# PSUM banks of attention from one list of free banks, with a new order of the attention words

## The chip, the cores and the metric

The kernel runs on one core of a Trainium2 chip. The metric is the device time of one execution in microseconds (us), the median of several runs; lower is better.

## What is computed

The reference chains three blocks on two sequences (B = 2) of S = 448 tokens with DM = 768 channels (12 heads of D = 64):

```python
scores = matmul(q, k^T) / sqrt(64); scores[j > i] = -1e9          # causal attention
attn = exp(scores - rowmax); attn = attn / (rowsum + 1e-9); x = attn @ v
h = relu(x^T @ w_tok1) @ w_tok2; u = x + h^T                      # mixing over tokens, 448 -> 256 -> 448
x = u + relu(u @ w_ch1) @ w_ch2                                   # MLP over channels, 768 -> 1536 -> 768
u = x + real(fft2(x)); un = normalised u                          # Fourier mixing
out = u + relu(un @ w_ch1b) @ w_ch2b                              # MLP, 768 -> 3072 -> 768
```

Inputs are 64-bit floats. The kernel turns each weight into a high and a low part (fp32r) and makes three matmuls for one product: high by high, low by high, high by low.

## The kernel before

The program has five stages; the change concerns the first, which holds the attention, the token mixing, the conversion of the first weights and the first six tiles of the first MLP. Its work is cut into 571 "words", a letter with numbers. The string `ORDER` lists them in one hand-written order, and `tc.manual_schedule` puts each word's instructions on its engines in just that order. Every engine takes its own instructions strictly in that order; between engines only data and buffers make one wait. The rest of the program has its own order and is not changed.

Heads are worked in 12 pairs n = 0 to 11; three pairs make a half (0 to 3). The words that this text speaks of:

- `K`n loads q and k of pair n, `V`n loads v, `R`k loads raw weight k, all as DMAs from SyncE's queue (SP). `e`n.p scales q (VectorE, pairs 0 to 2). `k`, `l`, `q`, `m` split k and q in high and low (pairs 3 and up).
- `S`n.g (scores, L350) makes one group of score rows of both heads on TensorE (PE) into two neighbouring PSUM banks. Pair 0 has four groups, the others three. `N`n.i (maxima, L379, VectorE) and `E`n.i (exps, L387, ScalarE) then work on row block i and read those banks. Group 0 of pairs 1 and up holds row blocks 0 and 1.
- `T`n.u (transposes, L400, PE, four small transposes into one bank), `C`n.u (pt_copy, L413: ScalarE for u = 1 and 3, VectorE else) brings them to SBUF; `P`n (pv, L419, PE) multiplies by v, `O`n (pv_copy, ScalarE), `X`n (rows, L439, PE transposes), `x`n (divide, L450, VectorE) writes the attention result of the pair into the tile `x32` of its half, of which there is one buffer for all halves.
- `h`, `g` split that result; `A`h.t (mix_in, PE, 12 matmuls), `r`, `s`; `B`h.p (channels, L504, PE) transposes pair p of half h out of `x32`, `b` copies it; `D`h.p (mix_out, PE, 6 matmuls), `d`, `u`, `w`.
- `W`k.j is step j of the conversion of weight k (0: ScalarE, 1 to 3: VectorE, 4: ScalarE, 5: GpSimd). `U`f (18 matmuls) and `Y`x (12) are tiles of the first MLP on PE, `y`, `z`, `a` read them.

PSUM has eight banks, the tile `psum`. In attention they are dealt out by two fixed rings, independent of what is free. `ybank` (L209) goes round banks 0 to 3 and serves T, P, X, A, B and D (and, two at a time by `ypair`, groups 2 and 3 of pair 0). `spair` (L217) alternates between banks 4, 5 and banks 6, 7 and serves all other S, and U and Y through `sbank`, which uses one of the two. A word that writes a bank waits until the last reader of that bank is done. After attention `bank` (L221) goes round all eight.

Of the kernel before, what the change touches and what calls it, by code (L numbers as in the profile page):

```python
# [70 lines left out]

ORDER = """K0 e0.0 S0.0 e0.1 K1 N0.0 E0.0 S0.1 N0.1 K2 S0.2 e1.0 N0.2 S0.3 N0.3 E0.1 e1.1 e2.0 S1.0 V0 N1.1
S1.1 E0.2 K3 E0.3 N1.0 T0.2 T0.4 T0.3 E1.0 E1.1 N1.2 E1.2 C0.2 T0.0 Z0 V1 T0.1 e2.1 C0.4 S1.2 C0.1 C0.0 k3
R0 S2.0 l3 C0.3 P0 N1.3 q3 E1.3 N2.1 K4 T1.0 S2.1 N2.0 E2.1 m3 Z1 O0 T1.2 C1.0 N2.2 T1.4 X0 E2.0 S2.2 E2.2
W0.0 T1.1 C1.2 C1.1 C1.4 q4 x0 S3.0 T1.3 N2.3 N3.1 C1.3 E2.3 P1 N3.0 E3.0 S3.1 T2.2 E3.1 O1 T2.0 k4 W0.1 R1
T2.4 S3.2 T2.3 m4 W1.0 N3.2 C2.2 T2.1 V3 C2.3 C2.1 l4 V2 C2.0 E3.2 C2.4 X1 N3.3 W0.2 W0.3 P2 S4.0 B0.0 E3.3
T3.2 O2 x1 K5 N4.0 T3.0 N4.1 T3.3 W0.4 C3.2 b0.0 S4.1 T3.4 C3.0 T3.1 E4.1 B0.1 W1.1 E4.0 C3.4 S4.2 C3.3 k5
C3.1 h0 Z2 P3 W0.5 X2 b0.1 q5 l5 g0 N4.2 N4.3 E4.2 m5 S5.0 E4.3 S5.1 x2 T4.3 Z4 W1.2 Z3 T4.4 C4.4 O3 h1 T4.1
h2 T4.0 C4.3 T4.2 C4.0 C4.2 N5.0 X3 K6 C4.1 k6 N5.2 N5.1 B0.2 g2 g1 R2 W2.0 q6 A0.1 A0.0 x3 V5 V4 W1.3 W2.1
E5.0 E5.1 S5.2 l6 m6 E5.2 S6.0 W1.4 K7 r0.0 N5.3 P4 E5.3 S6.1 N6.0 N6.1 s0.0 r0.1 b0.2 T5.4 O4 k7 s0.1 X4  # L80
T5.1 T5.0 C5.4 T5.2 E6.0 E6.1 x4 W1.5 D0.0 C5.1 D0.1 N6.2 C5.0 T5.3 W2.2 S6.2 E6.2 q7 h3 l7 m7 S7.0 d0.1
C5.2 K8 q8 C5.3 P5 N6.3 R3 k8 h4 N7.0 E6.3 N7.1 d0.0 T6.4 T6.2 T6.0 E7.0 E7.1 S7.1 S7.2 O5 T6.3 l8 g4 V6 K9
C6.3 k9 C6.2 C6.4 B1.1 X5 C6.0 T6.1 D0.2 N7.2 m8 q9 Z5 x5 N7.3 W2.3 b1.1 B1.2 C6.1 B1.0 P6 Z6 d0.2 E7.2 S8.0
N8.0 N8.1 h5 E7.3 T7.3 O6 b1.2 T7.0 b1.0 T7.2 C7.3 T7.4 T7.1 C7.0 X6 E8.0 E8.1 S8.1 S8.2 C7.1 W2.4 Z7 g5 g3
C7.2 A1.1 C7.4 A1.0 x6 N8.2 B2.0 N8.3 W3.0 W3.1 W3.2 E8.2 l9 m9 S9.0 E8.3 S9.1 V7 P7 V8 K10 r1.1 s1.1 u0.1
h6 W2.5 Z8 u0.0 r1.0 s1.0 N9.0 T8.0 W3.3 T8.1 b2.0 T8.3 q10 u0.2 k10 R4 W4.0 N9.1 E9.0 O7 X7 C8.1 C8.0 T8.4
E9.1 C8.3 D1.0 x7 B2.1 T8.2 N9.2 S9.2 m10 E9.2 l10 w0.1 S10.0 C8.4 d1.0 C8.2 P8 b2.1 N9.3 E9.3 T9.2 T9.1
D1.1 W3.4 O8 h7 K11 q11 T9.0 W4.1 N10.0 N10.1 W4.2 C9.2 T9.3 C9.1 T9.4 E10.0 C9.3 E10.1 d1.1 X8 C9.0 D1.2
S10.1 S10.2 m11 x8 h8 k11 C9.4 V9 P9 V11 Z9 u1.0 N10.2 E10.2 N10.3 E10.3 d1.2 O9 W3.5 l11 S11.0 S11.1 B2.2
R5 W5.0 b2.2 T10.1 C10.1 T10.0 T10.2 g7 g8 w0.2 w0.0 g6 N11.0 N11.2 N11.1 T10.3 C10.3 u1.2 E11.0 A2.0 r2.0  # L90
C10.2 C10.0 X9 T10.4 W4.3 A2.1 W5.1 x9 W5.2 W4.4 E11.1 S11.2 s2.0 V10 C10.4 P10 N11.3 u1.1 E11.2 r2.1 s2.1
E11.3 T11.2 C11.2 T11.0 C11.0 T11.1 O10 T11.4 T11.3 W5.3 C11.4 X10 W4.5 R6 W6.0 W6.1 Z10 R7 C11.1 C11.3 P11
w1.2 D2.0 O11 X11 x10 D2.2 d2.2 Z11 x11 h10 d2.0 B3.1 b3.1 u2.0 h9 W5.4 w1.1 w1.0 U0 g10 B3.2 U1 W6.2 u2.2
y0 b3.2 h11 B3.0 y1 W5.5 W7.0 W7.1 W6.3 W6.4 g9 g11 A3.0 A3.1 z0 D2.1 b3.0 r3.0 s3.0 W7.2 z1 W7.3 r3.1 s3.1
U2 y2 D3.0 D3.1 d3.0 z2 d3.1 W7.4 U3 W6.5 W7.5 w2.2 w2.0 d2.1 u3.0 u2.1 w3.0 w2.1 D3.2 y3 z3 u3.1 d3.2 Y0
w3.1 u3.2 w3.2 a0 Y1 a1
"""
# [7 lines left out]
def fused_kernel(ctx: ExitStack, tc: tile.TileContext, qk, v, w1, w2, wa, wb, wc, wd, fa, fb, out):  # L105
# [97 lines left out]

    def take(ring, n):
        k = turn[ring] % n
        turn[ring] += 1
        return k

    def ybank():  # L209
        return psum[:, take("y", 4)]  # L210

    def ypair():
        k = take("y", 4)
        take("y", 4)
        return psum[:, k : k + 2]

    def spair():  # L217
        k = 4 + 2 * take("s", 2)
        return psum[:, k : k + 2]
# [807 lines left out]
```

## Time and profile before

| | |
|---|---|
| median of 3 runs | 684.19 us (683.26 to 685.48) |
| the profiled execution | 683.87 us, span of its instructions 682.0 us |
| PE busy | 676.6 us, 99% of the span |
| VectorE (DVE) busy | 533.6 us, 78% |
| ScalarE (ACT) busy | 288.8 us, 42% |
| GpSimd (POOL) busy | 122.4 us, 18% |

The attention stage is the first 151 us or so of the span: its last matmuls are those of `Y1`, which start at 148.6 us. A matmul's record runs on past the start of the next one, since matmuls are pipelined; what a group of matmuls costs is therefore read from its first start to the first start of the group behind it. In the rows below, a word can be found by its line: L363 with L377 is S, L408 T, L425 P, L444 X, L489 A, L507 B, L520 D. L385 is N, L395 E, L417 C, L457 x, L343 V, L335 e, L154 W.3.

### The profile page before, as it was taken

To read this page: it belongs to the slowest core of one execution; us is meant where nothing else is said; L and a number is where in the kernel's file an instruction comes from. 1 tells how busy PE (TensorE), PEld (TensorE's weight loads), DVE (VectorE), ACT (ScalarE), POOL (GpSimd) and SP (SyncE) were. 2 spreads that over 40 slices of the span, in tenths; PEclk is the share of its full clock that TensorE was granted. 3 is DMA by queue.
4 is the path that set the end of the run, shared out by engine and by line. 5 is a ranking of instruction groups with operands and counts; after the bars stand their busy time and mean duration, and the time that the engine had idled before them with its cause. 6 is when DMAs were issued, how large, how long until landed. Compare 5 with 4: busy or idle time off the path is not lost.

```text
span 682.0 us, 10238 instructions
## 1 busy us (share of the span) xinstructions
PE 676.6 (99%) x3922; PEld 618.9 (91%) x3922; DVE 533.6 (78%) x888; ACT 288.8 (42%) x619; POOL 122.4 (18%) x102
## 2 busy tenths in 40 slices
...
PEclk9999999999999999999999999999999999999999
...
GB/s 226 113 128 116 115 88 63 78 213 142 131 152 110 109 125 92 93 1 1 93 93 94 125 153 93 99 90 151 124 93 93 175 113 145 93 92 76 111 46 55
DMA packets 20865, 73.38 MB, mean 108 GB/s; under 512 B 2366, under 2 KB 7230, under 8 KB 20448
## 3 DMA queue, kind: packets, MB, share of 16 engines
...
HBM read 69.96 MB, written 2.75 MB: 107 GB/s over the span
## 4 chain that ended last, share of the span: by engine, by line
PE 98%; DVE 1%; ACT 0%; DMA 0%; issue 0%; SPq 0%; DVEq 0%
PE psum L259 13%; PE psum L239 13%; PE psum L263 13%; PE psum L264 13%; PE psum L238 13%; PE psum L240 13%; PE psum L363 4%; PE psum L408 3%; PE psum L425 3%; PE psum L489 3%; PE psum L520 2%; PE psum L718 2%; PE psum L787 1%; PE psum L444 1%; PE psum L507 1%; PE psum L377 1%
## 5 line engine op out<-in xcount | busy, mean ns | idle before, releaser
L259 PE MATMUL psum<-gh,wh 128*128 128x448 f32 x432 | 157.5, 365 | 0.0
L239 PE MATMUL psum<-acth,wl 128*128 128x448 f32 x432 | 156.8, 363 | 0.0
L264 PE MATMUL psum<-gl,wh 128*128 128x448 f32 x432 | 156.6, 363 | 0.0
L263 PE MATMUL psum<-gh,wl 128*128 128x448 f32 x432 | 156.6, 362 | 0.0
L238 PE MATMUL psum<-acth,wh 128*128 128x448 f32 x432 | 156.6, 362 | 0.0
L240 PE MATMUL psum<-actl,wh 128*128 128x448 f32 x432 | 156.0, 361 | 0.0
L143 ACT ACTIVATE m<-w 128x512 f32<-128x512 f32 (+2 forms) x92 | 70.9, 772 | 121.0 <-DVE wl L163 87.0
L161 ACT CAST wh<-m 128x512 fp32r<-128x512 f32 (+1 forms) x90 | 63.3, 704 | 91.4 <-PE psum L264 55.3
L264 PEld LDWEIGHTS psum<-gl,wh 128*128 128x128 f32 x432 | 81.0, 188 | 6.0
L238 PEld LDWEIGHTS psum<-acth,wh 128*128 128x128 f32 x432 | 81.0, 188 | 5.9
L263 PEld LDWEIGHTS psum<-gh,wl 128*128 128x128 f32 x432 | 81.0, 188 | 5.7 <-issue 0.2
L259 PEld LDWEIGHTS psum<-gh,wh 128*128 128x128 f32 x432 | 81.1, 188 | 5.6 <-issue 0.2
L239 PEld LDWEIGHTS psum<-acth,wl 128*128 128x128 f32 x432 | 81.1, 188 | 5.0
L240 PEld LDWEIGHTS psum<-actl,wh 128*128 128x128 f32 x432 | 80.9, 187 | 5.2
L163 DVE TENSOR_TENSOR wl<-m,wh 128x512 fp32r<-128x512 f32 (+1 forms) x84 | 69.5, 830 | 14.0 <-ACT wh L161 13.7
L150 DVE SCALAR_TENSOR_TENSOR m<-w,m 128x512 uint32<-128x512 uint32 (+2 forms) x92 | 78.5, 853 | 2.2
L145 DVE TENSOR_SCALAR m<-m 128x512 f32<-128x512 f32 (+2 forms) x92 | 51.0, 554 | 36.9 <-ACT m L143 36.9
L154 DVE SCALAR_TENSOR_TENSOR m<-w,m 128x512 uint32<-128x512 uint32 (+2 forms) x92 | 78.1, 850 | 1.8
L244 ACT ACTIVATE gh<-psum 128x448 fp32r<-128x448 f32 x72 | 37.8, 540 | 74.1 <-PE psum L240 73.8
L246 DVE SCALAR_TENSOR_TENSOR gl<-psum,gh 128x448 fp32r<-128x448 f32 x72 | 43.8, 619 | 29.1 <-ACT gh L244 29.1
L395 ACT ACTIVATE p<-psum,nmx 112x112 f32<-112x112 f32 (+3 forms) x96 | 46.5, 502 | 10.2 <-DVE nmx L385 10.1
L146 DVE TENSOR_SCALAR m<-m 128x512 uint32<-128x512 uint32 (+2 forms) x92 | 48.0, 522 | 2.6
(160 smaller groups left out, 812.0 us busy)
## 6 DMA issues: line engine op xcount, KB each, us to landing
...
```

The source lines that it names most:

```text
L143: act.activation(out=m, in_=hi.bitcast(F32), func=AF.Abs)
L145: vec.tensor_scalar(out=m, in0=m, scalar1=F64_MIN, scalar2=F64_MAX, op0=ALU.max, op1=ALU.min)
L150: vec.scalar_tensor_tensor(out=mu, in0=lo, scalar=29, in1=mu, op0=ALU.logical_shift_right, op1=ALU.bitwise_or)
L154: vec.scalar_tensor_tensor(out=mu, in0=hi, scalar=0xC0000000, in1=mu, op0=ALU.bitwise_and, op1=ALU.bitwise_or)
L161: act.copy(wh, m)
L163: low_engine[0].tensor_tensor(out=wl, in0=m, in1=f(wh), op=ALU.subtract)
L238: mm(pb[:, :S], lhsT=lh, rhs=act_h[ct][b], start=ct == 0, stop=False)
L239: mm(pb[:, :S], lhsT=ll, rhs=act_h[ct][b], start=False, stop=False)
L240: tail[0] = mm(pb[:, :S], lhsT=lh, rhs=act_l[ct][b], start=False, stop=ct == NCT - 1).ins
L259: mm(pb[:, :S], lhsT=lh, rhs=gh, start=j + k == 0 and seeded is None, stop=False, skip_group_check=seeded is not None,)
L263: mm(pb[:, :S], lhsT=ll, rhs=gh, start=False, stop=False, skip_group_check=seeded is not None)
L264: tail[0] = mm(pb[:, :S], lhsT=lh, rhs=gl, start=False, stop=j == last and k == nk - 1, skip_group_check=seeded is not None,).ins
```

## The change

The two fixed rings go. One list, `ring`, holds the free banks in the order in which they came free. `grab` takes from it the bank that has been free for longest, with a preference: a single bank is looked for among banks 0 to 3 first and a pair (an even bank and its neighbour) among banks 4 to 7, where a bank of the other side counts as freed `FAR` = 4 places later. `drop`, called by the word that reads a bank last, puts it back at the end. All this happens while the program is written, in the order of the words: a bank counts as free as soon as its last reading word stands earlier in `ORDER`. U and Y now take one bank and not one of two. `bank`, after attention, goes round the eight banks in the order in which the list ends up.

`exps` drops the pair of its score group, `pt_copy` the bank of T, and so on for P, X, A, B, D, U and Y.

With it comes a new `ORDER` of the same 571 words. The diff, cut to its core (the lines of `ORDER` shown are those around the start, around P1 and P2, and around T4.2):

```diff
+FAR = 4
...
-ORDER = """K0 e0.0 S0.0 e0.1 K1 N0.0 E0.0 S0.1 N0.1 K2 S0.2 e1.0 N0.2 S0.3 N0.3 E0.1 e1.1 e2.0 S1.0 V0 N1.1
-S1.1 E0.2 K3 E0.3 N1.0 T0.2 T0.4 T0.3 E1.0 E1.1 N1.2 E1.2 C0.2 T0.0 Z0 V1 T0.1 e2.1 C0.4 S1.2 C0.1 C0.0 k3
...
-W0.0 T1.1 C1.2 C1.1 C1.4 q4 x0 S3.0 T1.3 N2.3 N3.1 C1.3 E2.3 P1 N3.0 E3.0 S3.1 T2.2 E3.1 O1 T2.0 k4 W0.1 R1
-T2.4 S3.2 T2.3 m4 W1.0 N3.2 C2.2 T2.1 V3 C2.3 C2.1 l4 V2 C2.0 E3.2 C2.4 X1 N3.3 W0.2 W0.3 P2 S4.0 B0.0 E3.3
...
-h2 T4.0 C4.3 T4.2 C4.0 C4.2 N5.0 X3 K6 C4.1 k6 N5.2 N5.1 B0.2 g2 g1 R2 W2.0 q6 A0.1 A0.0 x3 V5 V4 W1.3 W2.1
-E5.0 E5.1 S5.2 l6 m6 E5.2 S6.0 W1.4 K7 r0.0 N5.3 P4 E5.3 S6.1 N6.0 N6.1 s0.0 r0.1 b0.2 T5.4 O4 k7 s0.1 X4
...
+ORDER = """K0 K1 e0.0 S0.1 S0.0 e0.1 N0.1 N0.0 E0.1 S0.2 e1.1 e1.0 S0.3 N0.2 V0 E0.0 S1.1 N0.3 S1.0 E0.2 N1.2 E0.3 E1.2
+N1.0 K2 S1.2 T0.2 K3 N1.1 T0.4 T0.0 e2.1 T0.1 E1.0 C0.2 E1.1 e2.0 C0.1 T0.3 S2.1 C0.4 q3 C0.0 N1.3 C0.3 k3 S2.0
+m3 E1.3 P0 N2.2 Z1 T1.1 N2.0 T1.2 R0 T1.4 E2.2 l3 T1.0 O0 K4 V1 N2.1 X0 C1.2 E2.1 T1.3 E2.0 W0.0 C1.0 S2.2 C1.4
+C1.3 V3 Z0 x0 N2.3 q4 S3.0 S3.1 N3.0 N3.2 C1.1 E2.3 E3.2 P1 O1 T2.0 T2.1 W0.1 T2.4 h0 R1 k4 S3.2 T2.3 l4 N3.1
+E3.1 C2.0 C2.4 T2.2 C2.1 N3.3 C2.3 C2.2 X1 V2 K5 W0.2 m4 E3.0 E3.3 k5 P2 x1 T3.4 T3.3 Z2 T3.0 W1.0 B0.1 T3.1
...
+E4.0 Z3 P3 x2 E4.3 O3 V5 K6 W1.1 h2 S5.0 W0.5 S5.1 B0.0 b0.0 N5.1 T4.1 C4.1 g1 T4.3 k6 N5.0 q6 g2 N5.2 m6 X3 R2
+E5.1 E5.0 A0.1 A0.0 r0.1 T4.4 T4.0 V4 C4.3 W1.2 E5.2 B0.2 x3 r0.0 l6 W1.3 T4.2 W1.4 C4.4 S5.2 W2.0 C4.0 C4.2 K7
+s0.1 q7 S6.0 N5.3 R3 b0.2 s0.0 k7 W1.5 E5.3 N6.0 S6.1 Z4 l7 N6.2 P4 K8 m7 S6.2 D0.0 h3 N6.1 E6.2 T5.0 N6.3 T5.2
...
-    turn = dict(y=0, s=0, all=0)
+    ring = list(range(8))
+    turn = [0]
+    held = {}
...
+    def grab(key, uses=1, n=1):
+        old = {b: i + FAR * ((b < 4) == (n == 2)) for i, b in enumerate(ring)}
+        if n == 2:
+            old = {b: max(old[b], old[b + 1]) for b in range(0, 8, 2) if b in old and b + 1 in old}
+        b = min(old, key=old.get)
+        k = list(range(b, b + n))
+        for b in k:
+            ring.remove(b)
+        held[key] = k, [uses]
+        return psum[:, k[0]] if n == 1 else psum[:, k[0] : k[0] + 2]
+
+    def drop(key):
+        k, left = held[key]
+        left[0] -= 1
+        if not left[0]:
+            ring.extend(k)
+
     def bank():
-        return psum[:, take("all", 8)]
+        turn[0] += 1
+        return psum[:, ring[(turn[0] - 1) % 8]]
...
-            sp = c.sp[g] = spair() if n or g < 2 else ypair()
+            sp = c.sp[g] = grab(("S", n, g), 1 if g or not n else 2, 2)
...
+            drop(("S", n, g))
...
-            tv = c.tv[u] = ybank()
+            tv = c.tv[u] = grab(("T", n, u))
...
+            drop(("T", n, u))
```

## Rows read from the trace of the kernel before

**Rows 1.** The page, parts 1 and 2: PE's busy time, and its granted clock.

```profile
PE 676.6 (99%) x3922; PEld 618.9 (91%) x3922; DVE 533.6 (78%) x888; ACT 288.8 (42%) x619; POOL 122.4 (18%) x102
PEclk9999999999999999999999999999999999999999
```

**Rows 2.** All waits of PE: who waited for whom, us, times, longest.

```profile
PE psum L197 <- PEq L1014: 0.8, 1, 0.8
PE psum L363 <- DVE resid L335: 0.6, 1, 0.6
PE psum L363 <- DMA resid<-in_qk: 0.2, 1, 0.2
```

**Rows 3.** Stretches: length, busy PE, PEld, DVE, ACT, POOL (instructions), clock, DMA.

```profile
0.00:17.00 17.00, 15.41 (x130) 11.49 (x130) 12.09 (x30) 12.89 (x46) 4.17 (x15) 1.00 0.81 226
34.00:51.00 17.00, 17.00 (x154) 14.05 (x154) 15.81 (x29) 14.53 (x41) 8.69 (x7) 1.00 0.39 128
51.00:68.00 17.00, 17.00 (x162) 14.36 (x160) 13.71 (x25) 14.50 (x47) 3.55 (x3) 1.00 0.35 116
```

**Rows 4.** Timeline of PE (start, us, what): score groups alone, and one behind another.

```profile
23.61 0.41 PE L363 MATMUL psum<-kh,qh 64*112 64x336 f32 x2
...
24.37 1.36 PE L408 MATMUL psum<-ident,p 112*112 112x112 f32 x12
25.66 0.46 PE L363 MATMUL psum<-kh,qh 64*112 64x448 f32 x2
...
26.55 0.98 PE L408 MATMUL psum<-ident,p 112*112 112x112 f32 x8
27.37 0.60 PE L444 MATMUL psum<-ident,ots 128*112 128x128 f32 x4
...
73.47 0.41 PE L363 MATMUL psum<-kh,qh 64*112 64x336 f32 x2
...
74.11 0.44 PE L363 MATMUL psum<-kh,qh 64*112 64x448 f32 x2
...
79.78 0.38 PE L363 MATMUL psum<-kh,qh 64*112 64x256 f32 x2
...
80.70 0.39 PE L363 MATMUL psum<-kh,qh 64*112 64x336 f32 x2
...
81.42 2.11 PE L425 MATMUL psum<-pt,v 112*64 112x448 f32 x16
```

**Rows 5.** Timeline of PE: S1.0 and S1.1, then S5.0, S5.1 and T4.3.

```profile
7.13 0.81 PE L363 MATMUL psum<-resid,resid 64*112 64x112 f32 x8
...
8.77 0.82 PE L363 MATMUL psum<-resid,resid 64*112 64x336 f32 x4 [0.64 <-DVE resid L335]
...
38.60 0.49 PE L363 MATMUL psum<-kh,qh 64*112 64x256 f32 x2
...
39.75 0.60 PE L363 MATMUL psum<-kh,qh 64*112 64x336 f32 x2
...
40.69 2.13 PE L408 MATMUL psum<-ident,p 112*112 112x112 f32 x20
42.66 0.60 PE L444 MATMUL psum<-ident,ots 128*112 128x128 f32 x4
```

**Rows 6.** The load of v: timeline (V2's issue, P2's start), and all twelve landings.

```profile
23.72 0.33 SPq L343 DMA_DIRECT2D v<-in_v  x1
28.06 2.30 PE L425 MATMUL psum<-pt,v 112*64 112x448 f32 x16
DMA to landing us min/median/max: 2.5/4.3/5.6
```

**Rows 7.** Timeline of DVE: two C4, then x3, W1.3 and W2.1.

```profile
42.48 1.16 DVE L417 COPY pt<-psum 112x448 f32<-112x448 f32 x2
45.14 0.68 DVE L457 TENSOR_TENSOR x<-psum,ssum 112x512 f32<-112x512 f32 x1
45.74 1.08 DVE L154 SCALAR_TENSOR_TENSOR m<-w,m 128x896 uint32<-128x896 uint32 x1
46.73 0.56 DVE L145 TENSOR_SCALAR m<-m 128x768 f32<-128x768 f32 x1
```

**Rows 8.** Timeline of PE: B0.2, then A0.1 and A0.0 up to S5.2.

```profile
43.10 0.55 PE L507 MATMUL psum<-ident,x 112*128 112x112 f32 x4
43.41 0.94 PE L489 MATMUL psum<-xh,w1h 112*128 112x384 f32 x4
...
47.80 0.46 PE L363 MATMUL psum<-kh,qh 64*112 64x448 f32 x2
```

More of the change, by code (lines that the diff above doesn't have):

```diff
@@ L69 @@
 ENGINES = {getattr(mybir.EngineType, e) for e in ("PE", "DVE", "Activation", "Pool", "SP")}
-ORDER = """K0 e0.0 S0.0 e0.1 K1 N0.0 E0.0 S0.1 N0.1 K2 S0.2 e1.0 N0.2 S0.3 N0.3 E0.1 e1.1 e2.0 S1.0 V0 N1.1
-S1.1 E0.2 K3 E0.3 N1.0 T0.2 T0.4 T0.3 E1.0 E1.1 N1.2 E1.2 C0.2 T0.0 Z0 V1 T0.1 e2.1 C0.4 S1.2 C0.1 C0.0 k3
-R0 S2.0 l3 C0.3 P0 N1.3 q3 E1.3 N2.1 K4 T1.0 S2.1 N2.0 E2.1 m3 Z1 O0 T1.2 C1.0 N2.2 T1.4 X0 E2.0 S2.2 E2.2
-W0.0 T1.1 C1.2 C1.1 C1.4 q4 x0 S3.0 T1.3 N2.3 N3.1 C1.3 E2.3 P1 N3.0 E3.0 S3.1 T2.2 E3.1 O1 T2.0 k4 W0.1 R1
@@ L76 @@
-T2.4 S3.2 T2.3 m4 W1.0 N3.2 C2.2 T2.1 V3 C2.3 C2.1 l4 V2 C2.0 E3.2 C2.4 X1 N3.3 W0.2 W0.3 P2 S4.0 B0.0 E3.3
-T3.2 O2 x1 K5 N4.0 T3.0 N4.1 T3.3 W0.4 C3.2 b0.0 S4.1 T3.4 C3.0 T3.1 E4.1 B0.1 W1.1 E4.0 C3.4 S4.2 C3.3 k5
-C3.1 h0 Z2 P3 W0.5 X2 b0.1 q5 l5 g0 N4.2 N4.3 E4.2 m5 S5.0 E4.3 S5.1 x2 T4.3 Z4 W1.2 Z3 T4.4 C4.4 O3 h1 T4.1
-h2 T4.0 C4.3 T4.2 C4.0 C4.2 N5.0 X3 K6 C4.1 k6 N5.2 N5.1 B0.2 g2 g1 R2 W2.0 q6 A0.1 A0.0 x3 V5 V4 W1.3 W2.1
-E5.0 E5.1 S5.2 l6 m6 E5.2 S6.0 W1.4 K7 r0.0 N5.3 P4 E5.3 S6.1 N6.0 N6.1 s0.0 r0.1 b0.2 T5.4 O4 k7 s0.1 X4
@@ L81 @@
[L81 to L95, printed above, removed]
@@ L96 @@
-w3.1 u3.2 w3.2 a0 Y1 a1
+ORDER = """K0 K1 e0.0 S0.1 S0.0 e0.1 N0.1 N0.0 E0.1 S0.2 e1.1 e1.0 S0.3 N0.2 V0 E0.0 S1.1 N0.3 S1.0 E0.2 N1.2 E0.3 E1.2
[3 more added lines that the diff above has]
+E3.1 C2.0 C2.4 T2.2 C2.1 N3.3 C2.3 C2.2 X1 V2 K5 W0.2 m4 E3.0 E3.3 k5 P2 x1 T3.4 T3.3 Z2 T3.0 W1.0 B0.1 T3.1
@@ new lines @@
+C3.4 O2 h1 b0.1 C3.1 W0.3 C3.3 T3.2 C3.0 q5 W0.4 X2 S4.0 C3.2 N4.1 E4.1 S4.1 N4.2 m5 N4.0 l5 S4.2 g0 N4.3 E4.2
+E4.0 Z3 P3 x2 E4.3 O3 V5 K6 W1.1 h2 S5.0 W0.5 S5.1 B0.0 b0.0 N5.1 T4.1 C4.1 g1 T4.3 k6 N5.0 q6 g2 N5.2 m6 X3 R2
+E5.1 E5.0 A0.1 A0.0 r0.1 T4.4 T4.0 V4 C4.3 W1.2 E5.2 B0.2 x3 r0.0 l6 W1.3 T4.2 W1.4 C4.4 S5.2 W2.0 C4.0 C4.2 K7
+s0.1 q7 S6.0 N5.3 R3 b0.2 s0.0 k7 W1.5 E5.3 N6.0 S6.1 Z4 l7 N6.2 P4 K8 m7 S6.2 D0.0 h3 N6.1 E6.2 T5.0 N6.3 T5.2
+E6.0 O4 E6.3 E6.1 X4 T5.4 T5.3 d0.0 C5.2 x4 Z5 T5.1 C5.1 S7.2 C5.3 C5.0 S7.0 C5.4 k8 W3.0 S7.1 q8 P5 V6 D0.2
@@ new lines @@
+N7.3 N7.2 E7.3 O5 T6.4 l8 N7.0 E7.0 T6.1 E7.2 X5 m8 T6.2 T6.0 h4 W2.1 K9 d0.2 g3 V7 N7.1 x5 D0.1 u0.2 T6.3 k9
+C6.2 B1.2 C6.4 C6.0 B1.1 E7.1 d0.1 W2.2 W3.1 q9 g4 C6.1 Z6 b1.1 l9 C6.3 Z7 T7.3 P6 S8.2 b1.2 S8.0 h5 S8.1 C7.3
+u0.1 N8.3 g5 E8.3 A1.0 B1.0 K10 W2.3 V8 T7.0 O6 k10 W2.4 N8.1 N8.0 W3.2 r1.0 A1.1 N8.2 C7.0 T7.4 W2.5 u0.0 s1.0
+E8.2 m9 T7.1 C7.4 E8.1 E8.0 C7.1 X6 b1.0 q10 T7.2 R4 S9.2 S9.1 x6 r1.1 C7.2 P7 T8.2 N9.3 s1.1 l10 N9.2 T8.0 E9.3
+O7 K11 W3.3 T8.1 C8.2 C8.0 E9.2 X7 m10 C8.1 T8.4 T8.3 x7 C8.4 S9.0 N9.1 N9.0 S10.0 W4.0 S10.1 C8.3 W4.1 W3.4 P8
@@ new lines @@
+E9.1 E9.0 T9.2 h7 T9.0 w0.2 Z8 T9.4 N10.0 N10.2 O8 C9.0 E10.2 B2.0 E10.0 V9 C9.2 q11 C9.4 X8 D1.2 V11 W3.5 N10.1
+T9.1 W4.2 b2.0 g7 T9.3 D1.0 h6 d1.2 C9.3 C9.1 W4.3 x8 g6 k11 P9 l11 d1.0 S10.2 m11 h8 O9 S11.1 g8 S11.0 u1.2
+E10.1 N10.3 E10.3 N11.2 S11.2 A2.1 N11.3 N11.1 w0.0 Z10 E11.2 E11.3 T10.1 W4.4 T10.0 T10.4 T10.2 N11.0 R5 C10.2
+E11.0 C10.4 D1.1 T10.3 C10.1 C10.0 Z9 E11.1 A2.0 C10.3 w0.1 d1.1 V10 T11.1 r2.1 s2.1 u1.0 W5.0 P10 u1.1 T11.0
+r2.0 W5.1 T11.2 B2.1 T11.4 W5.2 w1.0 s2.0 C11.0 T11.3 C11.2 w1.1 b2.1 C11.4 B2.2 C11.1 W5.3 C11.3 P11 O10 W4.5
@@ L97 @@
+X9 x9 X10 b2.2 R6 D2.0 w1.2 Z11 W6.0 O11 W6.1 W5.4 W5.5 d2.0 D2.1 U0 R7 X11 W7.0 x10 D2.2 d2.1 h10 W6.2 h9 x11
+g9 W7.1 h11 W7.2 g10 W7.3 g11 U2 y0 U3 A3.1 r3.1 B3.2 y2 z0 A3.0 U1 s3.1 z2 r3.0 s3.0 d2.2 y3 W6.3 D3.2 z3 W6.4
+u2.2 u2.1 B3.0 D3.0 w2.1 y1 z1 b3.0 d3.0 b3.2 W6.5 B3.1 W7.4 d3.2 u3.0 u2.0 Y0 D3.1 w2.2 b3.1 w3.0 d3.1 u3.2
+u3.1 W7.5 a0 w2.0 w3.2 Y1 w3.1 a1
 """
@@ L202, in fused_kernel @@
     vec.memset(eps_t, EPS)
[L204 to L219, printed above, removed]
+    def grab(key, uses=1, n=1):
[13 more added lines that the diff above has]
+            ring.extend(k)
     def bank():
-        return psum[:, take("all", 8)]
+        turn[0] += 1
+        return psum[:, ring[(turn[0] - 1) % 8]]
     wide_pool = [None]
@@ L417, in pt_copy @@
             (act.copy if u in (1, 3) else vec.tensor_copy)(c.pt[:, u], c.tv[u][:TS, :S])
+            drop(("T", n, u))
         def pv(n):
             c = pairs[n]
-            c.ot = ybank()
+            c.ot = grab(("P", n))
             for j in range(NI):
@@ L433, in pv_copy @@
             act.copy(c.ots, c.ot[:, :S])
+            drop(("P", n))
         def divisors(n):
@@ L441, in rows @@
             c = pairs[n]
-            c.xp = ybank()
+            c.xp = grab(("X", n))
             for i in range(NI):
@@ L462, in divide @@
             )
+            drop(("X", n))
             if wrap:
@@ L484, in mix_in @@
             h = halves[n]
-            hp = mixed[n, t] = ybank()
+            hp = mixed[n, t] = grab(("A", n, t), 2)
             k = 0
```

21 lines of the change are left out of this document (14 added, 7 removed).

## Prediction

> **What bounds the kernel now.** The page comes first: PE is busy for 676.6 of 682.0 us and its granted clock is full in every slice [rows 1]. Then the waits of PE: 1.6 us in three waits over the whole span, 0.2 of it for a load, 0.8 ahead of the warm-up, 0.6 in S1.1 [rows 2]. No line tells of a bank. But a busy PE need not be PE at its peak: a stop shorter than a matmul's own latency hides inside its record. So the third view is the timeline of PE, read from first start to first start, and the fourth the stretches, which show how close the engines behind PE are to being the bound: in attention DVE is busy for 13.7 to 15.8 of 17 us and ACT for 14.5 [rows 3]. PE sets the time; in attention DVE and ACT have little to spare, so a stop of theirs reaches PE soon. After attention neither work nor order changes, and its bank ring is again eight deep; what attention gains or loses shifts the rest as a whole.
>
> **What the bank list can remove by itself: next to nothing.** The only stop that I find at a bank is S5.1, whose pair E4.3 frees. S5.0 takes 1.15 us to its successor where S9.0 takes 0.92, S5.1 0.94 to T4.3 where S3.1 took 0.76 to T2.2 [rows 4, 5]: 0.4 us together, of which S5.0's half is more likely a late low part of q. I let all 0.4 go: **-0.4** (0 to -0.4).
>
> **What the new order removes: visits to the score groups.** The list allows three pairs of banks in flight where the ring had two, so score groups can follow one another. Counted in the two orders: runs of neighbouring score groups on PE fall from 22 to 13; exits from a score group into transposes fall from 13 to 3, into pv from 8 to 7, and exits into A or D rise from 1 to 3; entries from transposes fall from 13 to 8, from pv from 5 to 4, from A or D from 3 to 0. Prices [rows 4]: S8.1 takes 0.64 us to S8.2, but S3.1 0.76 to T2.2 and S9.1 0.72 to P7: 0.12 and 0.08 for leaving. The 12 transposes at 24.37 take 1.29 us to S3.2; 20 at 40.69 take 1.97, or 0.0985 each [rows 5], so 12 should take 1.18: 0.11 more, nearly all of it for entering a score group, of which the first transpose after a score group has its share too (the 20 at 40.69 stand behind one as well). Ten exits at 0.12 to 0.17 are 1.2 to 1.7; one exit into pv 0.1; five entries at 0.09 0.5; the three entries from A or D against two exits into them I bound by one entry and one exit each, between -0.5 and +0.4, and take -0.1. Sum **-2.2** (-1.5 to -2.7). Nothing hides this: it lies on PE, which sets the time. PE's matmuls are otherwise the same.
>
> **The start.** S1.0 takes 1.64 us and S1.1 starts after 0.64 us of idling, for q's scaling on DVE, which stood behind N0.3 [rows 2, 5]. In the new order e1.1 and e1.0 stand ahead of N0.2, and this goes: 1.64 less the 0.92 of a group 0 [rows 4] is **-0.7**. Next late is the pair of S0.0, freed by E0.0 just ahead of S1.1; with S0.2 and S0.3 between I expect 0 to 0.3 back, and the bound is -0.4.
>
> **P2 and the load of V2.** V2 waits for P1, whose buffer it takes; it was issued at 23.72 when P1 had ended, and P2 started at 28.06, 4.34 us later, the median landing of a v being 4.3 [rows 6]. X1 took 0.69 to P2 where X3 took 0.44 to a transpose [rows 4 to 6]; with 0.09 for leaving the transposes PE lost 0.16 there. In the new order S3.1 moves ahead of P1, so PE has 0.76 less to do under that load and 0.05 less for the first transpose: the wait grows to 0.97, **+0.8**. If the load lands in 2.5 us it is hidden (-0.2), in 5.6 the wait is 2.3 (+2.1) [rows 6]; I take its own 4.3, since K5 and V2 are issued side by side as before. The other loads that move (V0 ahead of K2, V1 behind R0 and K4, R1 behind V3, R3 some 7 us earlier) have a K, V or R each to let past, under 1 us, and over 4 us until their first reader: nothing.
>
> **T4.2 and S6.0.** Working out the list word by word, T4.2 takes bank 1 from the free ones 4, 5 and 1: bank 4 is freed for longer, but being above 3 it counts four places later. Bank 1 was X3's, freed by x3 four words before. x3 writes the one buffer of `x32`, so it waits for B0.2, which still reads it, and B0.2 is the matmul word just ahead of T4.2. PE therefore finishes B0.2, waits for a whole x3, and goes on: 0.68 us [rows 7] and two hand-overs, **+0.9** (0.7 to 1.0). Before, A0.1 and A0.0, 4.39 us, stood between B0.2 and the next use of that bank and hid it [rows 8].
> On DVE W1.3, C4.4 and C4.0 are queued behind x3, and C4.0 frees the second bank of S6.0's pair. From x3's start: 0.60 to W1.3, 0.99 for it, then 1.16 for two copies [rows 7], 2.75. PE meanwhile has x3's 0.68, T4.2 with its exit, 0.48, and S5.2, 0.79: 1.95. S6.0 waits **+0.8** (0 to 1.0).
>
> **Small ones.** Elsewhere the list hands out a bank or E feeds a transpose with only one or two PE words between: S2.1 on E1.1, T5.4 on E6.3, P6 on C6.3, X8 on E10.2, A2.1 on E10.3. No row shows these; the nearest are the two of 0.2 at S5 [rows 5]. Five of 0.16 are **+0.8** (0 to 2.0). The tail (U, Y) has 2.4 to 3.6 us of matmuls between every hand-over: nothing.
>
> **Sum.** -0.4 - 2.2 - 0.7 + 0.8 + 0.9 + 0.8 + 0.8 = 0.0. Against the profiled execution that is 683.9; the median of the runs is 0.3 above it, so I forecast **684.2**. All bounds together give -2.8 to +4.4, which will not all fall one way.
>
> **The rivals.** A difference under 0.3%, 2.05 us, cannot be told from none here.
> 1. *The gain stays.* V2 lands in 2.5 us, S6.0's wait hides behind a DVE that is not late, and the small ones are 0.2: -0.4 - 2.2 - 0.7 - 0.2 + 0.9 + 0.2 = -2.4, **681.8**. For it: PE hardly waits anywhere in before [rows 2]. Against: T4.2 and V2 follow from the order alone. Chance 0.16.
> 2. *DVE becomes the bound, slower.* Between its words N5.2, m6 and x3 DVE has only m6 and W1.2, under 2 us, while PE does A0.1, A0.0, T4.4, T4.0 and B0.2, some 5.5. So DVE stands idle for about 2.7 us in front of x3, in a stretch in which it was idle for 1.2 [rows 3]. What it loses beyond that is work for the next 17 us, where it had 3.3 spare. If that spare lies in the wrong places, PE waits out the 2.7 once more: **686.9**. It decides from the point at which DVE's lag outlives S6.0, that is if T5 and S7 still wait for copies. Against: 0.8 of it is in my sum, and the spare is there. Chance 0.12.
> 3. *The list does not do what it says.* Three pairs in flight are of use only if the exps free them in time; if neighbouring score groups wait for a pair, the 2.2 is lost: **686.4**. Against: E of the pair before stands well ahead of nearly every S. Chance 0.03.
> 4. *The clock.* New short waits are sprinkled through attention; if PE's clock fell from 2.4 to 1.2 GHz between those of P2 and S6.0, 20 us of matmuls would take twice as long: **704**. The rows speak against it: with 1.6 us of the first 17 idle the granted clock reads 1.00 [rows 3]. Chance 0.01. The Trainium skill, "TensorE: Matmul & The Clock Gate", section on "A second HAM failure mode: psum-queue depth-cycling", tells of a kernel in which cycling through PSUM banks made PE idle in short pieces so that its clock swung; that is this rival, and this trace does not agree so far.
>
> **How the numbers follow.** The forecast has 0.68. Faster by over 0.3%: rival 1, 0.16. Slower: rivals 2 to 4, 0.16. Within: 0.68. The range for 8 in 10 takes in rival 1's time and most of rival 2's: 681.8 to 686.6.
>
> **What would show it.** Right: score groups in runs, with the transposes' stretches longer; no idling at S1.1; P2 starting some 4.4 us after P1's end, right behind the landing of V2; T4.2 starting 0.9 us late behind x3, and S6.0 0.8 behind C4.0. Wrong: T4.2 right behind B0.2; P2 right behind X1; PE waiting for pt copies after 60 us; a granted clock under 1; an attention stage that ends more than 2 us off 148.6 for Y1's start.

## The result, and the profile of the changed kernel

The changed kernel takes **688.16 us** (median of 6 runs, 687.94 to 688.75) where the kernel before, in 6 runs beside it, takes 684.08 (683.26 to 685.48): a ratio of 1.006, 95% interval 1.0047 to 1.0073. It is slower by 0.6%. The forecast was 684.2 with a range up to 686.6, and slower had a chance of 0.16: the prediction was wrong. Its profiled execution took 688.75 us, span 687.0.

First, where: the first matmul of `Y1` starts at 150.67 us where before it started at 146.37. (The 148.6 of the text ahead is the start of Y1's last matmul; in the changed kernel that is 152.90, the same 4.3 later.) So 4.3 us of the loss lie in attention; behind it the profiled executions differ by 0.7.

The page, part 1, then all waits of PE (who waited for whom: us, times, longest), as [rows 1, 2] show them for before:

```profile
PE 678.2 (99%) x3922; PEld 618.8 (90%) x3922; DVE 546.9 (80%) x888; ACT 288.6 (42%) x619; POOL 124.3 (18%) x102
PE psum L412 <- DVE actl L508: 1.3, 1, 1.3
PE psum L516 <- DVE pt L421: 0.9, 1, 0.9
PE psum L412 <- DVE x L463: 0.9, 1, 0.9
PE psum L197 <- PEq L1028: 0.8, 1, 0.8
PE psum L412 <- DVE pt L421: 0.3, 1, 0.3
PE psum L516 <- DVE x L463: 0.2, 1, 0.2
PE psum L450 <- ACT p L398: 0.2, 1, 0.2
PE psum L366 <- DVE pt L421: 0.2, 1, 0.2
```

Two things are new. PE waits for VectorE in six lines, and VectorE is busy for 13.3 us more with the same 888 instructions. The waits are, from the top: T11.3 behind s2.0, B1.2 behind C6.2, T4.2 behind x3 (the one that was forecast), T3.2 behind C3.4, B0.0 behind x2, X8 behind E10.2, S6 behind C4.4. Each of these is a wait for a bank: PE goes on 54 to 56 ns after the end of the word that reads the bank last. Read from first start to first start, against the length of the same word where it waits for nothing, all waits of attention sum to some 7.3 us in 16 places; before it was some 1.6 in 5. The difference is 5.7; Y1 is late by 4.3, so the words themselves became some 1.4 shorter.

The same stretches as in [rows 3] and one later (length, then busy us and instructions of PE, PEld, DVE, ACT, POOL, then clock and DMA):

```profile
34.00:51.00 17.00, 15.63 (x146) 13.12 (x146) 14.26 (x23) 13.14 (x42) 7.68 (x5) 1.00 0.34 107
51.00:68.00 17.00, 16.98 (x155) 13.57 (x154) 15.58 (x26) 15.76 (x50) 6.43 (x6) 1.00 0.38 123
102.00:119.00 17.00, 15.72 (x128) 12.96 (x128) 14.00 (x22) 12.54 (x36) 8.54 (x6) 1.00 0.10 40
```

The granted clock is full in these rows (1.00), so it is not that. VectorE does fewer instructions in 34 to 51 us than before (23 for 29) and is busy for 14.26.

**Why VectorE is busy for longer.** Groups of VectorE's instructions in the first 150 us, shapes kept apart (shapes, count | busy, mean ns | idle before). First the kernel before:

```profile
L417 DVE COPY pt<-psum 112x448 f32<-112x448 f32 x36 | 21.3, 618 | 5.5 <-PE psum L408 2.9 <-ACT p L395 1.5 <-ACT kh L322 0.8
L150 DVE SCALAR_TENSOR_TENSOR m<-w,m 128x768 uint32<-128x768 uint32 x4 | 3.8, 952 | 0.0
L437 DVE SCALAR_TENSOR_TENSOR ssum<-ssum 112x8 f32<-112x8 f32 x12 | 2.4, 196 | 0.4 <-ACT p L395 0.3
L464 DVE COPY x<-x 112x4 f32<-112x4 f32 x2 | 0.3, 172 | 0.1
```

and the changed kernel:

```profile
L421 DVE COPY pt<-psum 112x448 f32<-112x448 f32 x36 | 20.8, 612 | 2.7 <-PE psum L412 2.5
L150 DVE SCALAR_TENSOR_TENSOR m<-w,m 128x768 uint32<-128x768 uint32 x4 | 5.3, 1324 | 0.0
L443 DVE SCALAR_TENSOR_TENSOR ssum<-ssum 112x8 f32<-112x8 f32 x12 | 4.5, 373 | 0.7 <-ACT p L398 0.7
L471 DVE COPY x<-x 112x4 f32<-112x4 f32 x2 | 2.8, 1382 | 0.1
```

The copies out of PSUM take what they took (612 and 618 ns). Operations between tensors of SBUF take longer, a copy of 112x4 elements eight times as long. The timeline of the two worst places (start, us, engine, what; in brackets the idle time before it) shows beside what. T11.3's wait:

```profile
111.87 1.31 POOL L544 TENSOR_TENSOR actl<-resid,acth 128x448 fp32r<-128x448 f32 x1
112.21 1.38 DVE L146 TENSOR_SCALAR m<-m 128x768 uint32<-128x768 uint32 x1
113.14 2.13 POOL L163 TENSOR_TENSOR wl<-m,wh 128x768 fp32r<-128x768 f32 x1
113.63 2.46 DVE L150 SCALAR_TENSOR_TENSOR m<-w,m 128x768 uint32<-128x768 uint32 x1
115.23 1.85 POOL L544 TENSOR_TENSOR actl<-resid,acth 128x448 fp32r<-128x448 f32 x1
116.01 0.54 DVE L508 SCALAR_TENSOR_TENSOR actl<-psum,acth 128x384 fp32r<-128x384 f32 x1
116.48 1.67 DVE L421 COPY pt<-psum 112x448 f32<-112x448 f32 x3
116.61 0.59 PE L412 MATMUL psum<-ident,p 112*112 112x112 f32 x4 [1.28 <-DVE actl L508]
```

and B1.2's:

```profile
66.09 1.31 POOL L483 TENSOR_TENSOR xl<-x,xh 112x512 fp32r<-112x512 f32 x1 [3.35 <-ACT xh L477]
66.58 1.95 DVE L471 COPY x<-x 112x4 f32<-112x4 f32 x1
67.35 1.15 POOL L329 TENSOR_TENSOR kl<-resid,kh 128x448 fp32r<-128x448 f32 x1
68.44 1.67 DVE L421 COPY pt<-psum 112x448 f32<-112x448 f32 x3
69.11 1.13 PE L516 MATMUL psum<-ident,x 112*128 112x112 f32 x8 [0.90 <-DVE pt L421]
```

In the second, x5's copy of 112x4 elements is on VectorE from 66.58 to 68.53. That is the time of two GpSimd instructions, g4 and l9, back to back, which end at 67.40 and 68.50; the same copy before took 0.17, with no GpSimd instruction beside it. C6.2 is queued behind it on VectorE, holds B1.2's bank, and PE waits. In the first, W5.2 (L150) starts at 113.63 and ends at 116.09, which is 0.82 after GpSimd's W4.5 (113.14 to 115.27); elsewhere W5.2 takes 0.95 in all. s2.0 is queued behind it and holds T11.3's bank. The copies of 116.48, out of PSUM, run beside a GpSimd instruction (115.23 to 117.08) and take 1.67 for three, as at 68.44.

Taking from each VectorE record of attention the shortest one of its operation and shape, and summing what exceeds 0.1 us, gives 14.8 us in 19 instructions (before: 1.1 in 3). All 19 overlap a GpSimd instruction; none of them reads PSUM. I call this VectorE *held by GpSimd*. The 13.7 us more of it account for the 13.3 us that VectorE is busy for longer.

### The profile page after: what moved, and what is told of

The parts are those of the page before. It is cut to its first block, busy times and chain, and to the rows that moved or that the text cites. A ratio compares the mean times of both kernels' runs of the same rounds, so it can differ in the third digit from the quotient of the medians.

```text
span 687.0 us, 10218 instructions
## 1 busy us (share of the span) xinstructions
PE 678.2 (99%) x3922; PEld 618.8 (90%) x3922; DVE 546.9 (80%) x888; ACT 288.6 (42%) x619; POOL 124.3 (18%) x102
## 4 chain that ended last, share of the span: by engine, by line
PE 94%; DVE 4%; ACT 1%; issue 1%; DVEq 0%
PE psum L262 13%; PE psum L242 13%; PE psum L266 13%; PE psum L267 13%; PE psum L241 13%; PE psum L243 12%; PE psum L366 3%; PE psum L430 2%; PE psum L496 2%; PE psum L412 2%; PE psum L530 2%; PE psum L732 2%; PE psum L801 1%; DVE nmx L388 1%; DVE pt L421 1%
## 5 line engine op out<-in xcount | busy, mean ns | idle before, releaser
L150 DVE SCALAR_TENSOR_TENSOR m<-w,m 128x512 uint32<-128x512 uint32 (+2 forms) x92 | 80.0, 870 | 2.3
L154 DVE SCALAR_TENSOR_TENSOR m<-w,m 128x512 uint32<-128x512 uint32 (+2 forms) x92 | 79.1, 861 | 1.8
L146 DVE TENSOR_SCALAR m<-m 128x512 uint32<-128x512 uint32 (+2 forms) x92 | 51.6, 560 | 2.7
L398 ACT ACTIVATE p<-psum,nmx 112x224 f32<-112x224 f32 (+3 forms) x96 | 46.8, 512 | 9.9 <-DVE nmx L388 9.8
```

What stands on the lines that cost most here:

```text
L146: vec.tensor_scalar(out=mu, in0=mu, scalar1=3, scalar2=0x3FFFFFF8, op0=ALU.logical_shift_left, op1=ALU.bitwise_and)
L150: vec.scalar_tensor_tensor(out=mu, in0=lo, scalar=29, in1=mu, op0=ALU.logical_shift_right, op1=ALU.bitwise_or)
L154: vec.scalar_tensor_tensor(out=mu, in0=hi, scalar=0xC0000000, in1=mu, op0=ALU.bitwise_and, op1=ALU.bitwise_or)
```

## The experiments

Theory 1: the changed order puts GpSimd's instructions beside VectorE's SBUF operations; VectorE comes late to its PSUM copies, and the list has handed out banks that wait for just those. Theory 2: it is the list or the order on PE themselves, and VectorE's lateness is only seen beside it. "Held" below is the sum just described, Y1 the start of its first matmul; both are from the one profiled execution of each kernel (that of spread took 685.38 us, 2.0 above its median). Each ratio is to the kernel before in runs beside it.

| kernel | median us | ratio (95% interval) | held us | Y1 |
|---|---|---|---|---|
| before | 684.08 | | 1.1 | 146.4 |
| the change | 688.16 | 1.006 (1.0047 to 1.0073) | 14.8 | 150.7 |
| no_pool_new | 682.01 | 0.9976 (0.9965 to 0.9987) | 0.1 | 144.4 |
| no_pool_old | 685.16 | 1.0015 (1.0005 to 1.0024) | 0.3 | 147.9 |
| no_pool_x2 | 680.15 | 0.9941 (0.9926 to 0.9956) | | 142.5 |
| old_order_list | 688.61 | 1.006 (1.0045 to 1.0075) | 2.2 | 150.8 |
| pick | 688.11 | 1.0056 (1.0041 to 1.0071) | | 150.2 |
| spread | 683.41 | 0.9998 (0.9985 to 1.0011) | 6.1 | 146.5 |
| spread2 | 684.27 | 1.0001 (0.9993 to 1.001) | 6.3 | 146.4 |
| spread3 | 686.59 | 1.0026 (1.0013 to 1.0039) | | 147.7 |
| search_list | 690.45 | 1.0096 (1.0076 to 1.0117) | 10.5 | 150.5 |
| search_ring | 692.8 | 1.0126 (1.0111 to 1.0141) | 6.0 | 153.5 |

### Without GpSimd: no_pool_new and no_pool_old

The low parts that GpSimd computes in attention are left out, in the changed kernel and in the kernel before; PE reads the high part in their place, so it has the same matmuls. The result lacks those low parts. The diff is cut to two of the places:

```diff
-            (pool if n else vec).tensor_tensor(out=c.kl, in0=c.k32, in1=f(c.kh), op=ALU.subtract)
+            c.kl = c.kh
...
-            pool.tensor_tensor(out=h.l[:, :, sl], in0=h.x[:, :, sl], in1=f(h.h)[:, :, sl], op=ALU.subtract)
+            pass
```

> The changed kernel without GpSimd's work in attention: the low parts of k, of the attention result, of the first MLP's input for the first sequence and of the first eight weights are left out, and PE reads the high part in their place, so its matmuls are as many and as long. Theory 1 (the new order lays GpSimd's words beside VectorE's operations on SBUF, which then stand still, and the banks come back late): VectorE's 14.8 us of stretched instructions in attention go, with them the waits of T3.2, B0.0, B1.2 and T11.3 (some 3.5 us), T4.2's 1.0 stays; about 684.5 us. Theory 2 (the list deals out banks whose reader stands late in the order, whatever VectorE's pace): the waits stay, 687 or more.

> The control: the same work of GpSimd left out of the kernel before. Theory 1: only 1.1 us of VectorE's attention instructions were stretched there, so at most 0.7 us is won: 683.4 to 684.1. Theory 2 expects the same. A gain of 3 us or more here would mean that GpSimd's words cost time by something other than the overlap with VectorE.

With the new order leaving them out gives 6.2 us back and puts the kernel ahead of before. With the old order it gives nothing: 685.16 misses the expected 683.4 to 684.1, for Y1 now waits 1.15 us for ScalarE at the end of attention, and S0.2 and S0.3 take 0.6 longer; elsewhere no more than 0.4 is won, at S5. PE waited for no GpSimd word in the changed kernel, and for no load, so what came back came through VectorE.

The 6.2 are a difference of medians. Y1 is 6.2 earlier too, but 0.8 of that lies in S0.2 and S0.3, which take 2.48 us in the changed kernel's profiled execution and 1.67 here, with no GpSimd instruction between 4 and 10 us. In the changed kernel S0.2's matmuls of 336 columns still go at half pace (they start 0.65 us apart, those of S1.1 0.34, though the granted clock reads 1.00 for both), and PE reaches its full pace at a different point in each profiled execution: but for search_ring's, the two words take 1.7 to 2.7 us in them. So what the traces show of the holding is nearer 5.4. What PE still waits for in no_pool_new:

```profile
PE psum L419 <- DVE x L470: 0.8, 1, 0.8
PE psum L199 <- PEq L1035: 0.8, 1, 0.8
PE psum L373 <- DMA resid<-in_qk: 0.3, 1, 0.3
PE psum L373 <- DVE pt L428: 0.2, 1, 0.2
```

T3.2's, B1.2's and T11.3's waits are gone, with the same order and the same banks. T4.2's behind x3 and S6's behind C4.4 stay: 0.95 at T4.2, 0.83 at S6.0 and S6.1, against the forecast's 0.9 and 0.8. This kernel is what the prediction costed; the time of the changed kernel is this plus the holding. Theory 1 had set 684.5, so 2.5 more than it expected came back: besides the four waits that it named, those at A0.1, X8, D1.2, T5.3, S4.1 and a few smaller ones are gone too (about 1.8), and so is the 0.8 of the first words.

### The forecast term alone: no_pool_x2

```diff
-                h.x = ap.tile([TS, NI, XW], F32, tag="x32", name="x32", bufs=1)
+                h.x = ap.tile([TS, NI, XW], F32, tag="x32", name="x32", bufs=2)
```

no_pool_new with two buffers for `x32`, so that x3 need not wait for B0.2. (The second buffer was not run with GpSimd's low parts in place.)

> As the run of the changed kernel without GpSimd's work (682.0), and with a second buffer for the tile x32, so that x3 needn't wait for B0.2. If T4.2's wait of 0.95 us is the wait for x3 behind B0.2, and S6.0's and S6.1's 0.8 the copies queued behind it on VectorE, all three go: 680.3. If the bank is only freed late for another reason, 682.0 again.

1.9 us less, as expected, and of PE's waits only the warm-up's 0.8 and one of 0.2 for a load are left. So the mechanism at T4.2 and S6.0 was read rightly ahead of the result, and its price too.

### The list without the new order, and another bank for two words: old_order_list and pick

old_order_list has the changed kernel's list with the order of before. pick gives T11.3 and B2.2 banks that were free for long (bank 4 had been free for 5.9 us when T11.3 waited for its own; it ranked behind because of `FAR`):

```diff
+PICK = {("T", 11, 3): 4, ("B", 2, 2): 6}
...
-        b = min(old, key=old.get)
+        b = PICK.get(key, min(old, key=old.get))
```

> The list of free banks alone, with the order of before. Theory 1: GpSimd and VectorE meet as seldom as before, so no more than some tenths are lost: 684 to 685. Theory 2: the list costs by itself, PE waits right behind readers (T0, X1, T4, B1.1): some 3 us more than before, 687.

> The changed kernel with two banks chosen by hand: T11.3 takes bank 4, free for 5.9 us when it waited, in place of bank 0, and B2.2 takes bank 6. If T11.3's wait of 1.4 us is a loss of its own (theory 2), 686.7. If VectorE, held up by GpSimd, is what PE waits for in that place (theory 1), the wait moves to P11, which needs the copies, and the time stays within 0.5 of 688.2.

old_order_list is as slow as the change: theory 1 falls as the whole story, and theory 2 is right for this kernel in the places that it named, with 1.6 more than its 687. VectorE is held for 2.2 us only. PE waits at banks, 3.9 us by the words' lengths:

```profile
PE psum L411 <- ACT p L397: 1.1, 1, 1.1
PE psum L515 <- ACT pt L420: 1.0, 1, 1.0
PE psum L449 <- ACT pt L420: 0.5, 2, 0.3
PE psum L411 <- DVE pt L420: 0.3, 1, 0.3
```

T0.0 waits for the exps E1.2, B1.1 for the copy C6.3, X1 and X8 and T4.0 for others. The list calls a bank free as soon as its last reader stands earlier in the order of the words. PE, however, reaches the next word when it has done its own, and the reader's engine may be far from there. The old order, written for rings of four and of two pairs, often has a reader only one or two words ahead of a writer to which the list then gives its bank. So the list has a cost by itself, and an order has to be made for it; the new order was, as no_pool_new shows, if VectorE keeps its times.

pick took T11.3's 1.44 us away and its median is the change's (688.11): P11 then waits for C11.0 and C11.2, which VectorE does late for the same reason (1.07 us at P11). Theory 1 expected that for this place: a better bank moves the wait to the data.

### GpSimd's words spread out: spread, spread2, spread3

spread keeps PE's words in their order and each on its bank, and keeps the whole computation. 133 of the 571 words, VectorE's operations on SBUF, GpSimd's and some loads and splits, stand elsewhere, so that by the trace's durations the two engines' SBUF work falls beside each other less. Around T11.3 (the first line is the changed kernel's):

```diff
-u1.0 W5.0 P10 u1.1 T11.0 r2.0 W5.1 T11.2 B2.1 T11.4 W5.2 w1.0 s2.0 C11.0 T11.3 C11.2 w1.1 b2.1 C11.4 B2.2 C11.1 W5.3 C11.3 P11 O10 W4.5
+W5.1 T11.1 r2.1 s2.1 V10 u1.0 P10 u1.1 T11.0 r2.0 T11.2 w1.1 B2.1 W5.2 W4.5 T11.4 s2.0 C11.0 w1.0 T11.3 C11.2 b2.1 W5.3 C11.4 B2.2 C11.1 C11.3 P11 O10
```

> The changed kernel with all its work, the same order of PE's words and the same bank for each; 133 of the 571 words are moved by some places, all of them VectorE's words on SBUF, GpSimd's words, the splits of k and q and the loads, so that GpSimd's operations fall beside other work. Theory 1 (GpSimd holds VectorE up): VectorE's stretched instructions in attention fall from 14.8 to under 4 us, T3.2, B1.2 and T11.3 no longer wait, about 683.5. Theory 2 (the banks alone): as the changed kernel, 687 to 688.

4.8 us of the 6.2 come back with the same list, the same banks and the same work on every engine. Moving 133 words also changes in what order VectorE does its own; but in no_pool_new no word moved, and the two together leave the holding as what made the change slow. Held time fell to 6.1 us only (under 4 was expected). Of PE's waits T4.2's stays (1.0), B1.2 is down to 0.39, T11.3's is gone, and one is new, 1.07 at A0, which waits for GpSimd's g2. The timeline of GpSimd and VectorE there (start, us, what):

```profile
39.83 2.98 POOL L482 TENSOR_TENSOR xl<-x,xh 112x512 fp32r<-112x512 f32 x1 [2.04 <-PE psum L411]
40.58 1.08 DVE L149 SCALAR_TENSOR_TENSOR m<-w,m 128x896 uint32<-128x896 uint32 x1
41.58 1.24 DVE L442 SCALAR_TENSOR_TENSOR ssum<-ssum 112x8 f32<-112x8 f32 x1
```

Here it is GpSimd that is held: g2 takes 2.98 us where it takes 1.29 elsewhere, and ends 1.15 after W1.2 (L149) of VectorE, although its record starts 0.75 ahead of W1.2's; then Z3 (L442), of 112x8 elements, is held until g2 ends at 42.81. spread2 moves W1.2 behind Z3 and m6; spread3 also puts T4.2 behind S5.2, so that S5.2 lies beside x3 (spread's order, then spread3's):

```diff
-... A0.1 q6 W1.2 Z3 m6 A0.0 W1.3 ... B0.2 x3 r0.0 T4.2 C4.4 S5.2 W1.5 ...
+... A0.1 q6 Z3 m6 W1.2 A0.0 W1.3 ... B0.2 x3 r0.0 C4.4 S5.2 T4.2 W1.5 ...
```

> The run spread with one word of VectorE moved: W1.2 from ahead of Z3 and m6 to behind them, off the GpSimd word g2. In spread A0 waited 1.07 us for g2, which took 2.98 us beside W1.2 where it takes 1.29 alone. GpSimd and VectorE hold each other up: g2 takes about 1.3 us, A0's wait falls under 0.2, T4.2 keeps its wait of 1.0 behind x3, time 683.4 - 0.9 = 682.5. No such hold (g2 is slow for another reason): A0 waits as before, 683.4.

> spread2 with T4.2 put behind S5.2, so that S5.2's 0.8 us lie beside x3 and T4.2 finds its bank free. Nothing but the order of the list costs T4.2 its wait: T4.2 waits 0, S6.0 0.3 to 0.6 for C4.0 behind x3, one more visit to the score groups costs 0.2: 682.5 - 1.0 + 0.4 + 0.2 = 682.1. VectorE sets the time there: S6.0 takes over the whole wait, 682.5.

In spread2 g2 takes 1.29 again and A0 waits no more, so the hold works both ways:

```profile
40.03 1.29 POOL L482 TENSOR_TENSOR xl<-x,xh 112x512 fp32r<-112x512 f32 x1 [2.03 <-PE psum L411]
```

The time did not fall: 684.27 where 682.5 was expected. In the profiled execution P1 is 0.73 longer: K3's load landed at 19.55 us (18.54 in spread), ScalarE idled 0.62 for it, and C1.1, which P1 needs, came late behind. S6.0 waits 0.46. So a microsecond won was lost again in that execution, where loads and copies have no slack left.

spread3 is a miss: T4.2's wait is gone, S5.2 now has one of 1.41, and the time is 2.3 us longer than spread2's. The last row is a stretch, read as in [rows 3].

```profile
46.20 0.54 ACT L397 ACTIVATE p<-psum,nmx 112x336 f32<-112x336 f32 x1
46.88 0.98 PE L365 MATMUL psum<-kh,qh 64*112 64x448 f32 x2 [1.34 <-ACT p L397]
...
47.87:51.28 3.41, 3.41 (x29) 2.81 (x26) 1.63 (x3) 2.13 (x4) 1.77 (x2) 0.50 0.43 170
```

I had taken S5.2's pair for free. Its pair is the one that E5.2 reads, and the first half of E5.2 ends at 46.74, just ahead of S5.2's start. In spread S5.2 starts at 48.43, long after, since PE stood at T4.2 for x3; with T4.2 moved away the next wait came out.

That wait alone is only 0.5 longer than the one that it replaces (from B0.2 to the next word 1.89 us, 1.40 in spread2). The larger part of the 2.3 seems to be the clock: after PE had stood for 1.34 us, the granted clock read 0.50 from 47.87 to 51.28, the lower of its two levels, 1.2 GHz for 2.4. T4.2 and S6.0, which lie in that stretch, take 0.92 and 1.67 us where spread has 0.53 and 0.90. Of the eight runs, the five with a mean clock of 0.997 or 0.998 take 686.0 to 687.7, the others 684.35, 684.57 and 686.85. That the wait brought the clock down is likely and not shown; in spread2 PE idles 0.9 us at T4.2 and the clock stays.

### Orders from a search: search_list and search_ring

Both have an order found by laying out all words on their engines with durations from the traces, with the list and with the rings (the first line of search_list's):

```diff
-ORDER = """K0 K1 e0.0 S0.1 S0.0 e0.1 N0.1 N0.0 E0.1 S0.2 e1.1 e1.0 S0.3 N0.2 V0 E0.0 S1.1 N0.3 S1.0 E0.2 N1.2 E0.3 E1.2
+ORDER = """K0 e0.0 S0.0 S0.1 K1 e0.1 N0.0 E0.0 N0.1 e1.1 e1.0 S0.2 S0.3 N0.2 N0.3 S1.1 E0.1 E0.2 N1.2 S1.0 E0.3 N1.0 E1.2 R0
```

> The list of the change with an order in which every kind of word was moved by a search over many orders, with the durations of the rows and with GpSimd and VectorE kept apart on SBUF (theory 1 as a rule of the search). If both causes are as said, attention ends some 5 us earlier than in the kernel before: 679 to 680. If an order can't gain what the list promises, 684.

> The two fixed rings of before with an order found in the same way. If the rings themselves forbid the gain, it stays at 683 to 684. If the order is what counts, 680.

Both miss every time that was expected, by 6 to 13 us. In search_list S2.0 waits for pair 2's load, which the search had moved too late, and others follow:

```profile
PE psum L365 <- DMA resid<-in_qk: 2.7, 1, 2.7
PE psum L365 <- ACT p L397: 1.5, 1, 1.5
```

Behind the wait of 2.7 us the granted clock reads 0.50 from 16.0 to 19.4 us, and P0, which lies there, takes 3.3 us where it takes 2.0 in the kernel before: the clock has a part in this loss too. An order packed tight on fixed durations has no slack for a load that lands later or a VectorE that is held. In search_ring the waits are at banks and data all through attention, with VectorE held for 6.0 us. It says nothing against rings, only against this search.

## Why the prediction was wrong, by its own steps

The step that failed is the one on the small ones: +0.8 (0 to 2.0), worked out with every engine at its durations of before, and with nothing for GpSimd's words, which moved too. The waits that belong there came to some 5.4 us, mostly because VectorE was held by GpSimd for 14.8. The steps one by one:

- **Bank waits at S5, -0.4: right in part.** In the changed kernel S5.0 waits for nothing. In S5.1 the second head still starts 0.16 us after the first, behind the second half of E4.0, which reads its bank; that is within the bounds of 0 to -0.4.
- **Visits to the score groups, -2.2: right.** Y1 is 4.3 later and waits are 5.7 more, so the words became some 1.4 shorter; S0.2 and S0.3 are 0.5 longer in this execution, by PE's pace at the start, and without them it is 1.9, in the bounds of 1.5 to 2.7. no_pool_x2, where PE hardly waits, says the same: Y1 is 3.9 earlier than before, 1.6 of it by the waits of before and 0.1 by S0.2 and S0.3, and 2.2 are left.
- **The start, -0.7: right.** S1.1's wait for q's scaling is gone. Nothing comes late in its place: the pair of S0.0 costs S1.1 no wait.
- **V2 and P2, +0.8: wrong in size.** V2 was issued at 23.75 and landed at 26.73, 3.0 us later and not 4.3, and P2 started at 27.16 without a wait. The median landing was taken for a load whose own landings vary from 2.5 to 5.6 [rows 6]; the bound of -0.2 was the result.
- **T4.2 and S6.0, +0.9 and +0.8: right.** 1.02 at T4.2, 0.83 at S6.0 and S6.1 in the changed kernel; no_pool_x2 shows both to be x3 behind B0.2. The rows that answer to [rows 7, 8]:

```profile
46.41 0.55 PE L516 MATMUL psum<-ident,x 112*128 112x112 f32 x4
47.06 0.69 DVE L463 TENSOR_TENSOR x<-psum,ssum 112x512 f32<-112x512 f32 x1 [2.16 <-PE psum L516]
47.81 0.60 PE L412 MATMUL psum<-ident,p 112*112 112x112 f32 x4 [0.86 <-DVE x L463]
```

- **Small ones, +0.8 (0 to 2.0): the step that failed.** The places named there, with T5.3 and D1.2 that wait for the same exps, are worth about 1.1 (S2 0.31, T5.3 0.23, X8 and D1.2 0.56), which is within that step's range. But T11.3 (1.44), B1.2 (1.06), T3.2 (0.50), A0.1 (0.32), B0.0 (0.31) and others not named add 4.3. The step looked for banks whose reader stands one or two *PE words* ahead, with every engine at its durations of before. It did not ask whether VectorE would keep those durations.
- **What was missing altogether** is a term for GpSimd. [rows 1] have it at 18% and no wait of PE named it, so its words were moved at nothing. The profile of before held the evidence: its timeline of GpSimd and VectorE (start, us, what) has

```profile
31.95 2.38 POOL L163 TENSOR_TENSOR w1l<-m,w1h 112x1024 fp32r<-112x1024 f32 x1 [4.84 <-ACT w1h L161]
33.47 1.35 DVE L145 TENSOR_SCALAR m<-m 128x896 f32<-128x896 f32 x1
35.18 1.32 POOL L326 TENSOR_TENSOR kl<-resid,kh 128x448 fp32r<-128x448 f32 x1 [0.84 <-ACT kh L322]
35.93 0.59 DVE L437 SCALAR_TENSOR_TENSOR ssum<-ssum 112x8 f32<-112x8 f32 x1
```

  The first of VectorE's takes 1.35 us where an operation of the same size takes 0.63 one step later (L146), and ends 0.5 after GpSimd's; the second takes 0.59, where the eleven others of its kind take 0.16 or 0.17, and ends with GpSimd's, at 36.5. (The first is the only one of its form and so not in the 1.1 us above.) The order of before kept such meetings rare. The diff shows that `W`, `g`, `l`, `Z` and `m` all move, and a meeting could have been bounded by the GpSimd instruction's length, 1.2 to 2.4 us in these rows.
- **Rival 2, VectorE becomes the bound, 686.9, was the nearest**, and the changed kernel shows its sign (VectorE idles 2.16 us in front of x3, where 2.7 was said). But its mechanism was idling in front of x3, and that was no more than the 1.9 of the two terms above: without GpSimd the same idling is there (2.93 us) and the kernel takes 682.01. The lateness came from held instructions, not from idle time. Rivals 3 and 4 did not occur in the changed kernel; the fall of the clock that rival 4 feared did come, for 3.4 us, in spread3 and in search_list.

The bounds, too, were added up wrongly: those stated give -3.3 to +4.2 and not -2.8 to +4.4. The +4.1 is just inside, but by a term that they do not hold.

Put together: the terms that were named give 682.0 without GpSimd (the forecast's own terms, without the +0.8 for V2 and the small ones, would have been 682.6), and the holding gives +6.2, of which some tenths may be the start of the program. The old order shows no loss to GpSimd, so the comparison ends at +4.1.
